# Early value products, block 1's x transposed by DMA, q's weights loaded once: a transformer block on one core

## The chip, the core and the metric

The kernel runs on one core of one Trainium2 chip. The metric is device time in microseconds (us) of one execution; lower is better. A run with more than 1.5% over the fastest of its kernel counts as slow and is left out of comparisons. "Profile" below is one execution recorded by the hardware profiler; its span is a little shorter than the device time of the same execution (731.3 for 733.04 us in the main one below). Engines: PE (TensorE, matmuls), DVE (VectorE), ACT (ScalarE), POOL (GpSimd), SP (SyncE, here only issuing transfers).

## The reference, cut to what matters

```python
x  = A_x                                   # 1 x 2048 x 1024, bf16
xn = layernorm(x)
qkv = xn @ wqkv                            # 1024 x 3072, 32 heads of 32
# position s attends to s, s-2, ..., s-14   (W, dil = 8, 2), masked below 0
s  = attention(q, k, v) @ wo
h  = silu(xn @ w1) * (xn @ w3)             # 1024 -> 3584
g  = silu(h @ w2)                          # 3584 -> 1024
return x + s * g
```

## The kernel before

The 2048 positions are four **blocks** (0 to 3) of 512, and two of them make a half (b = 0, 1). Every large product is one level of a Strassen-like scheme, seven products in place of eight, so operands have to be summed and differenced first, on DVE. The program is written in dependency order with priorities; a scheduler fixes each engine's order when the kernel is built, and each engine works through its own list in that order.

The order of the main parts: layer norm and transposes of x; q, k, v of half 0; q, k, v of half 1; up-projection, down-projection and output projection of half 0 ("am", "da" to "de", "wa" in the profile); then the same of half 1. Attention of the four blocks is DVE work that the scheduler fits in beside PE.

The start, with block 1's transposes on PE (`ln_tp`) and copied out by ACT:

```python
b12 = k4("b12", (KH, CH), BF16)
x_load(2)
ln_dve(1, [0, 1])
ln_dve(1, [2, 3])
...
def tp1(*sts):
    for st in sts:
        ln_tp(1, st, [(b12[:].unsqueeze(1), slice(0, 1)), (xT[:, 2:3], slice(1, 2))])

for t, (w0, w1_, ws) in enumerate(((wq0, wq1, sq), (wk0, wk1, sk))):
    first_two(f"f{t}", ...,                # the first two of the seven products
              *((lambda: None, 4) if t == 0 else (lambda: tp1(2, 3), 0)))
    if t == 0:
        tp1(0, 1)
qkv_sums(wq0, wq1, sq)
xn_sums(xT[:, 0], xT[:, 1], b12[:], xT[:, 2], xs)     # needs block 1 transposed
```

```python
def c22(gp):                               # after each of two groups of product "de"
    sp5 = k4(f"dsp{b}_{gp}")
    act_copy(sp5[:], pe[gp][:])
    with hp():
        anchor["v"] = nc.vector.tensor_add(sp5[:], pb[gp][:], sp5[:])
        silu(g_tile(b, 1, 1, gp), sp5[:])

product(pe, lst(s1), rhs, True, c22)
product(pe, lst(s4), rhs, False, c12)      # accumulates on top of what c22 copied out
```

The second product on `pe` may not write a group before ACT has copied that group out. In ACT's queue, group 0's silu, which needs DVE's sum, stands before group 1's copy.

## Time and profile before

| what | before |
|---|---|
| device time, three runs | 733.41 us median (731.72 to 733.42) |
| span of the profile, granted clock | 730.3 us, 0.998 |
| PE busy | 714.2 us, 98% |
| PE's first q product to its first "eq" product | 13.25 to 29.57 us |
| half 1's up-projection starts ("am") | 529.79 us |
| last output projection starts ("wa") | 699.88 us |

How to read it: PE is the engine to shorten. This is the timeline of the kernel before, all engines, of the half-1 down-projection (start, length, engine, line, operation, output<-inputs, shape, count; in brackets the idle time ahead of it and what ended it):

```profile
649.13 1.17 POOL L387 COPY vT<-vT 128x64 bf16<-128x64 bf16 x1 [16.27 <-DVE BC L465]
650.60 0.77 POOL L401 DMA_DIRECT2D vT<-v_dram  x1 [0.30 <-POOL vT L387]
...
658.30 1.23 DVE L465 TENSOR_TENSOR oT<-Ep,vT 128x2048 bf16<-128x2048 bf16 x1 [4.65 <-DMA vT<-v_dram]
...
675.70 12.25 PE L149 MATMUL de<-wring,h_sb 128*128 128x512 bf16 x54
...
678.35 1.22 DVE L814 TENSOR_TENSOR dsp<-db,dsp 128x1024 f32<-128x1024 f32 x1
...
679.60 1.06 ACT L777 ACTIVATE h_sb<-dsp 128x1024 bf16<-128x1024 f32 x1 [8.73 <-DVE dsp L814]
680.57 0.99 ACT L159 COPY dsp<-de 128x1024 f32<-128x1024 f32 x1
```

PE runs the second "de" product from 675.70 without a break: 54 of its 56 matmuls are recorded (one record is missing in each group of 28). The first group's last matmul starts 27 x 0.216 = 5.83 us later, at 681.53, and the second group is due one pitch after it, at 681.75 us; ACT's copy of that group ends at 680.57 + 0.99 = 681.56. So no wait is recorded, yet the **slack**, the time between "free" and "due", is only 0.19 us.

### The profile page before, as it was taken

To read this page: it belongs to the slowest core of one execution; us is meant where nothing else is said; L and a number is where in the kernel's file an instruction comes from. 1 tells how busy PE (TensorE), PEld (TensorE's weight loads), DVE (VectorE), ACT (ScalarE), POOL (GpSimd) and SP (SyncE) were. 2 spreads that over 40 slices of the span, in tenths; PEclk is the share of its full clock that TensorE was granted. 3 is DMA by queue.
4 is the path that set the end of the run, shared out by engine and by line. 5 is a ranking of instruction groups with operands and counts; after the bars stand their busy time and mean duration, and the time that the engine had idled before them with its cause. 6 is when DMAs were issued, how large, how long until landed. Compare 5 with 4: busy or idle time off the path is not lost.

```text
span 730.3 us, 8739 instructions
## 1 busy us (share of the span) xinstructions
PE 714.2 (98%) x3312; PEld 345.8 (47%) x3367; DVE 624.2 (85%) x677; ACT 314.5 (43%) x328; POOL 99.3 (14%) x159
## 2 busy tenths in 40 slices
PE   7999999999999999999999999999999999999996
PEld 4655665654444444444444444444444444444442
DVE  7994688878798879878989899969859999979984
ACT  5744343437554546654545411123454555120233
POOL 0000000010400110142202010010345000510011
PEclk9999999999999999999999999999999999999999
DMA  9379148877756452467755745549799453666505
GB/s 321 140 177 286 57 147 281 254 210 262 200 204 231 143 175 87 141 194 242 231 174 191 240 156 186 178 162 375 188 283 326 136 159 102 192 190 203 179 5 111
DMA packets 117610, 140.82 MB, mean 193 GB/s; under 512 B 14273, under 2 KB 91073, under 8 KB 116929
## 3 DMA queue, kind: packets, MB, share of 16 engines
q1 hardware_dynamic: 103984, 101.47, 44.9%
q0 software_dynamic: 13584, 38.81, 17.2%
q8 instruction: 26, 0.43, 0.3%
q14 instruction: 16, 0.12, 0.1%
HBM read 98.30 MB, written 38.80 MB: 188 GB/s over the span
## 4 chain that ended last, share of the span: by engine, by line
PE 71%; DVE 18%; DMA 4%; issue 3%; ACT 3%; SPq 1%; POOL 0%; DVEq 0%; ACTq 0%; POOLq 0%
PE bm L149 17%; PE am L149 11%; PE em L149 11%; PE db L149 7%; PE bq L149 5%; PE de L149 4%; DVE pt L410 4%; PE eq L149 4%; PE da L149 3%; PE aq L149 3%; PE wb L149 2%; DVE pt L412 2%; PE we L149 2%; PE wa L149 2%; DMA q_dram<-pk 1%
## 5 line engine op out<-in xcount | busy, mean ns | idle before, releaser
L149 PEld LDWEIGHTS <-wring 128*128 128x128 f16 (+1 forms) x1920 | 201.7, 105 | 216.4 <-issue 5.2
L149 PEld LDWEIGHTS <-h_sb 128*128 128x128 f16 (+1 forms) x1088 | 114.0, 105 | 121.7 <-issue 1.0
L149 PE MATMUL bm<-xs,wring 128*128 128x512 f16 x504 | 117.3, 379 | 0.5 <-DVE h_sb L661 0.3
L149 PE MATMUL am<-xT,wring 128*128 128x512 bf16 x322 | 78.8, 379 | 0.9
L410 DVE TENSOR_TENSOR pt<-qt,kT 128x4096 bf16<-128x4096 bf16 x32 | 73.2, 2288 | 0.7
L149 PE MATMUL db<-wring,h_sb 128*128 128x512 f16 x336 | 73.2, 379 | 0.0
L465 DVE TENSOR_TENSOR BC<-Ep,vT 128x2048 bf16<-128x2048 bf16 x56 | 67.0, 1218 | 0.2
L646 DVE TENSOR_TENSOR um<-em,um 128x1024 f32<-128x1024 f32 x28 | 34.2, 1222 | 19.9 <-PE em L149 12.9
L648 ACT ACTIVATE g<-um 128x1024 bf16<-128x1024 f32 x28 | 29.6, 1057 | 49.7 <-DVE um L646 49.7
L149 PE MATMUL da<-wring,h_sb 128*128 128x512 bf16 x219 | 48.9, 379 | 0.3
L451 POOL DMA_DIRECT2D Ep<-pb x64 | 37.9, 600 | 25.5 <-DVE pb L447 18.5
L149 PE MATMUL bm<-h_sb,wring 128*128 128x512 f16 x168 | 39.7, 379 | 0.0
L149 PE MATMUL em<-xs,wring 128*128 128x512 f16 x168 | 39.7, 379 | 0.0
L412 DVE TENSOR_TENSOR pt<-pt 128x2048 bf16<-128x2048 bf16 x32 | 39.1, 1221 | 0.5
L475 DVE TENSOR_TENSOR oT<-oT,BC 128x2048 bf16<-128x2048 bf16 x32 | 39.1, 1220 | 0.5
L149 PE MATMUL em<-xT,wring 128*128 128x512 bf16 x161 | 39.2, 379 | 0.3
L159 ACT COPY bm<-am 128x1024 f32<-128x1024 f32 x28 | 28.0, 999 | 26.1 <-PE am L149 26.1
L159 ACT COPY pm<-em 128x1024 f32<-128x1024 f32 x28 | 28.4, 1013 | 19.3 <-PE em L149 19.2
L159 ACT COPY um<-bm 128x1024 f32<-128x1024 f32 x28 | 28.4, 1013 | 18.6 <-PE bm L149 18.2
L667 ACT CAST g<-bm 128x1024 bf16<-128x1024 f32 x28 | 28.3, 1010 | 17.6 <-PE bm L149 17.6
L351 DVE TENSOR_TENSOR pk<-eq,uq 128x1024 bf16<-128x1024 f32 x12 | 14.7, 1222 | 23.7 <-PE eq L149 13.2
L661 DVE TENSOR_TENSOR h_sb<-bm,pm 128x1024 bf16<-128x1024 f32 x21 | 25.6, 1218 | 5.3 <-PE bm L149 5.3
(176 smaller groups left out, 965.3 us busy)
## 6 DMA issues: line engine op xcount, KB each, us to landing
wring<-in_B_w_dram SPq DMA_DIRECT2D x61, 512.0 KB, 4.4
wring<-t_dram SPq DMA_DIRECT2D x16, 512.0 KB, 5.1
t_dram<-wring POOLq DMA_DIRECT2D x14, 512.0 KB, 4.5
wring<-in_A_wqkv_dram SPq DMA_DIRECT2D x6, 1024.0 KB, 8.0
wring<-t_dram SPq DMA_DIRECT2D x16, 384.0 KB, 5.5
wring<-in_B_w_dram SPq DMA_DIRECT2D x12, 384.0 KB, 4.7
wring<-in_A_x_dram SPq DMA_DIRECT2D x16, 256.0 KB, 6.1
Ep<-pb POOLq DMA_DIRECT2D x64, 64.0 KB, 4.9
```

Source lines behind the costliest of these rows:

```text
L149: anchor["pe"] = nc.tensor.matmul(ps, lhsT=lhs[k], rhs=rhs[k], start=(first and k == 0), stop=(k == n - 1), skip_group_check=not first,)
L159: nc.scalar.copy(out=out_, in_=in_)
L351: anchor["v"] = nc.vector.tensor_add(d, ps[:], a[0][:])
L410: nc.vector.tensor_mul(p_t[:], q[:], kT[:, :, o:o + CH])
L412: nc.vector.tensor_add(p_t[:, 0:4, :], p_t[:, 0:4, :], p_t[:, 4:8, :])
L451: nc.gpsimd.dma_start(out=pr[c][r:P:NR, :, sq * P:(sq + 1) * P], in_=pb[sq * 32:(sq + 1) * 32, :, :])
L465: nc.vector.tensor_mul(dst, E[:, w, :].unsqueeze(1).to_broadcast([P, n, CH]), vT[:, js, o:o + CH])
L475: nc.vector.tensor_add(A, A, B if w0 else C)
L646: v = nc.vector.tensor_add(su2[:], pe[:], su2[:])
L648: nc.scalar.activation(out=hl["g"][:, :, CH:], in_=su2[:], func=ACTF.Silu)
L661: anchor["v"] = nc.vector.tensor_add(h[:, :, CH:], pb[:], sp5[:])
L667: nc.scalar.copy(out=hl["g"][:, :, 0:CH], in_=pb[:])
```

## The change

Intent: give PE the transposes of block 1 back (they go to DMA, straight from normalised rows to both halves of the transposed x), and fill the time in which DVE still waits for them with the first two value products of half 0. For that v's weights must be loaded at the start; they then stay until half 1. So do q's, which saves loading those a second time (6 loads of 1 MB of q, k and v weights where there were 8; v's were loaded once before too). The core of the diff:

```diff
-    def qkv_sums(w0, w1_, st):
+    def qkv_sums(w0, w1_, st, again=False):      # again: three sums where four were
@@ park: block 1's q, k, v go to DRAM on POOL's queue
-            nc.sync.dma_start(out=dst, in_=tl[:])
+            (nc.gpsimd if c == 1 else nc.sync).dma_start(out=dst, in_=tl[:])
@@ scores: block 0's scratch lies in oT
-            sc[c] = att_tile((W, CH), BF16, f"Es{c}"), att_tile((NJ, CH), BF16, f"pt{c}")
+            sc[c] = att_tile((W, CH), BF16, f"Es{c}"), oT[:, 0] if c == 0 else att_tile((NJ, CH), BF16, f"pt{c}")
@@ slots of the weight ring, in the order in which the up-projection takes them
-    free = [0, 1, 2, 3, 4, 6, 7, 8, 9]
+    free = [8, 9, 0, 1, 4, 2, 3, 6, 7]
@@ start
+    wve = [att_tile((4, D), BF16, f"wve{h}") for h in I]
+    vsn = att_tile((2, 2, CH), FP32, "vsn")
-    b12 = k4("b12", (KH, CH), BF16)
+    b12 = rows(12, 2).rearrange("p (k n) -> p k n", k=KH)
+    TPE = ()                                     # row groups transposed on PE: none
+    qkv_load(2, 0, wve[0][:])
+    for st in range(NST):
+        ln_dve(1, [st])
+        if st not in TPE:
+            for a, d in ((0, b12), (1, xT[:, 2])):
+                nc.sync.dma_start(
+                    out=d[:, :, st * P:(st + 1) * P], in_=xt[1][:, st, a * CH:(a + 1) * CH], transpose=True,
+                )
+        if st == 1:
+            qkv_load(2, 1, wve[1][:])
     x_load(2)
-    ln_dve(1, [0, 1])
-    ln_dve(1, [2, 3])
...
-    for t, (w0, w1_, ws) in enumerate(((wq0, wq1, sq), (wk0, wk1, sk))):
+    snap += [vsn[:, 0], vsn[:, 1]]
+    for t, (w0, w1_, ws) in enumerate(((wq0, wq1, sq), (wk0, wk1, sk), (wve[0][:], wve[1][:], sk))):
...
-    qkv_seven(2, 0, *wv, sv, step0)
+    qkv_seven(2, 0, *wv, sv, step0, snap[4:6])
...
-    wq0 = qkv_load(0, 0, slot(8, (4, D)))
-    wq1 = qkv_load(0, 1, rows(0, 4).rearrange("p (k n) -> p k n", k=4))
-    qkv_sums(wq0, wq1, sk)
+    qkv_sums(wq0, wq1, sk, True)
```

More of the change, by code (lines that the diff above doesn't have):

```diff
@@ L315, in qkv_sums @@
         s3 = hi(w0.bitcast(FP16))
+        if again:
+            nc.vector.tensor_sub(s2, a22, s3)
+            nc.vector.tensor_add(s1, s2, a11)
+            nc.vector.tensor_sub(s4, a12, s2)
+            pace["owed"] += 3.4
+            return
         nc.vector.tensor_add(s1, a21, a22)
@@ L993, in tp1 @@
         for st in sts:
-            ln_tp(1, st, [(b12[:].unsqueeze(1), slice(0, 1)), (xT[:, 2:3], slice(1, 2))])
-    for t, (w0, w1_, ws) in enumerate(((wq0, wq1, sq), (wk0, wk1, sk))):
+            ln_tp(1, st, [(b12.unsqueeze(1), slice(0, 1)), (xT[:, 2:3], slice(1, 2))])
+    snap += [vsn[:, 0], vsn[:, 1]]
+    for t, (w0, w1_, ws) in enumerate(((wq0, wq1, sq), (wk0, wk1, sk), (wve[0][:], wve[1][:], sk))):
         first_two(f"f{t}", [qkv_A(w0, w1_, ws, g) for g in range(2)], B0[0], B0[1],
                   snap[2 * t:2 * t + 2], [qkv_copy(t, 0, 2 * g) for g in range(2)],
-                  *((lambda: None, 4) if t == 0 else (lambda: tp1(2, 3), 0)))
-        if t == 0:
-            tp1(0, 1)
+                  *((lambda: None, 4) if t == 0 else (lambda: None, 0)))
+    tp1(*TPE)
     qkv_sums(wq0, wq1, sq)
-    xn_sums(xT[:, 0], xT[:, 1], b12[:], xT[:, 2], xs)
+    xn_sums(xT[:, 0], xT[:, 1], b12, xT[:, 2], xs)
     qkv_sums(wk0, wk1, sk)
@@ L1012 @@
     tr(2)
-    wv = [slot(2 + 4 * h, (4, D)) for h in I]
+    wv = [wve[h][:] for h in I]
     sva = slot(0, (2, 4, CH), FP16)
@@ L1019, in before_v @@
         if g == 0:
-            for h in I:
-                qkv_load(2, h, wv[h])
             tr(3)
-        else:
             with behind("v"):
```

## The prediction

> **What bounds the kernel now.** I read the page first, its busy shares and slices, then the table of stretches, then PE's own waits, then the timeline of the first 75 us, the only place where the change moves much.
>
> ```profile
> PE 714.2 (98%) x3312; PEld 345.8 (47%) x3367; DVE 624.2 (85%) x677; ACT 314.5 (43%) x328; POOL 99.3 (14%) x159
> ...
> PE   7999999999999999999999999999999999999996
> ...
> DMA  9379148877756452467755745549799453666505
> ```
>
> PE is at 9 in every slice but the first and the last. DVE is full in places (49.28 of 50.00 us from 420 to 470), but PE is at 49.90 there, so DVE fills PE's time without setting it. PE's waits over the whole run, as the waits view names them:
>
> ```profile
> PE tp L280 <- DVE wring L254: 2.3, 1, 2.3
> PE warm L141 <- DVE warm L138: 1.3, 1, 1.3
> PE am L149 <- ACT bm L159: 0.7, 1, 0.7
> PE eq L149 <- DVE xs L294: 0.5, 1, 0.5
> PE zp L425 <- DVE dsu L823: 0.5, 1, 0.5
> PE bq L149 <- DVE pk L351: 0.3, 1, 0.3
> PE bm L149 <- DVE h_sb L661: 0.3, 1, 0.3
> ```
>
> That is all there is to recover by waiting less: about 3.6 us at the start (two rows the change doesn't touch), some 2.5 us elsewhere. The rest of any gain must come from PE work removed. The chain of waits is no guide here: from 143 us on it runs through transfers and DVE, while PE is busy for 37.77 of the 39.00 us from 143 to 182. So the question is what PE does between 13 and 40 us:
>
> ```profile
> 13.25 7.07 PE L149 MATMUL af<-xT,wring 128*128 128x512 bf16 x32
> 20.15 1.06 PE L280 MATMUL tp<-ident,wring 128*128 128x128 bf16 x16
> 21.04 3.62 PE L149 MATMUL af<-xT,wring 128*128 128x512 bf16 x15
> 24.50 1.06 PE L280 MATMUL tp<-ident,wring 128*128 128x128 bf16 x16
> 25.40 3.62 PE L149 MATMUL af<-xT,h_sb 128*128 128x512 bf16 x16
> 29.57 2.35 PE L149 MATMUL eq<-xs,h_sb 128*128 128x512 f16 x10 [0.54 <-DVE xs L294]
> ```
>
> The columns are start, length, engine, line, operation. One row of q products (32), one half of block 1's transposes, half of k's products (16; one record is missing), the other transposes, the rest of k's, and then a wait for the differences of x (xs), which need the transposed block 1.
>
> **What the Trainium skill says.** "TensorE: Matmul & The Clock Gate", Part 4 (PE-mode transpose): a transpose on TensorE is a matmul against the identity whose output lands in PSUM, so a copy must follow; about 275 ns in one kernel's context. The trace shows the copies (eight on ACT, about 0.6 us each) but not the price: 219 ns for one, and pipelined 0.89 us for sixteen by their starts (20.15 to 21.04), 56 ns each. "DMA: Bandwidth & Descriptors", Latency and other measured facts: a DMA transpose at 261 GB/s in one kernel. Agrees: from 60.7 to 62.7 us the later blocks' transposes alone move 271 GB/s; one of 256 KB takes 1.32 us to issue and 3.0 to 8.2 us to land. The same page, Issuing engines are not separate DMA queues: issuing from another engine saves only sequencer time. Here that is what is wanted: SP's queue is held for 29.3 us in six waits for DVE pk before 100 us, and what stands behind such a wait is held too. "SBUF — State Buffer", SBUF: two separate sides: while DVE runs in a two-port mode GpSimd can't write descriptors, so DMAs issued there may start late. The trace shows no harm: POOL's t_dram DMAs land in 4.5 us, SP's 512 KB weight loads in 4.4.
>
> **The change, part by part.** The instruction orders of the two builds give the counts.
>
> (a) Block 1's transposes leave PE: 3367 matmuls become 3335, the 3248 of 128x512 stay. 0.89 + 0.90 (24.50 to 25.40) = 1.79 us off PE's stream, all on the path. ACT loses the eight copies, 4.9 us, off the path.
>
> (b) First v products placed early: 32 matmuls (A11 B11 and A12 B21 for two groups) move to before the first eq products. Count unchanged; what they do is cover the wait for xs. The matmul pitch is 0.216 us (eight from 33.59 to 35.32). Before: 64 products x 0.216 = 13.82, plus 1.79, leaves 16.32 - 15.61 = 0.71 us lost between 13.25 and 29.57. That is the 0.54 of the view and a pipeline refill. After: 96 x 0.216 = 20.74, so eq would start at 13.25 + 20.74 = 34.0 us; the like point before is 29.57 + 32 x 0.216 = 36.5. Gain of (a) and (b) 2.5 us, if nothing new waits.
>
> (c) What must be there in time. DVE's order up to the first xs holds one more 128x2048 operation (pitch 1.14 us) and one bn_stats (0.6) less than before, so xs L294 comes about 0.5 us later, 28.8 instead of 28.29; each of the next three takes 1.13. DMA: the seven loads of 1 MB (x0, wq twice, x1, wk twice, v's first half) at the 390 GB/s of the timeline end near 2.2 + 18.4 = 20.6 us. Then a half of the transposes (0.5 MB at about 215 to 271 GB/s, 2.2 us), v's second half (2.7 us), the other half of the transposes: about 28 us, landing by 30. v's second half lands near 27 and is needed at 13.25 + 80 x 0.216 = 30.5; xs is done at 31 and needed at 34. Margins of 3 us, on estimates. The DMA queues were idle in these microseconds before (1 GB/s from 28 to 38 us), which is why I believe them.
>
> (d) PSUM. In the new ACT order the two q copies that free the first two accumulators stand behind a k copy which waits for k's third group of eight, done at 13.25 + 56 x 0.216 = 25.3. Copies of about 0.95: k until 26.3, q until 27.3. The first v product is due at 27.1 and needs that accumulator: 0.3 us of wait.
>
> (e) q and v weights loaded once, four of q's sums rebuilt with three: 2 MB less traffic at 112 to 122 us, and one DVE operation (1.14 us) less. Neither engine is the bound there; PE loses 0.27 us from 110 to 143. Worth 0 to 0.2 us.
>
> (f) Block 1's parks move to POOL's queue, b12 leaves the small pool: DVE's 6.4 us wait at 62 us for a k_dram landing should go, and with it PE's 0.3 at 65 us. Worth 0.3 us.
>
> (g) The reordered slot list, the scores' scratch in oT, v's snapshot in the attention pool: no PE work. They move DVE's fill-in work a few operations and could cost or give half a microsecond where act tables load (PE loses 1.2 us from 143 to 182).
>
> Sum: -1.8 - 0.7 + 0.3 - 0.3 = -2.5, and 0.1 back for (g): 733.4 - 2.4 = 731.0 us.
>
> **The rivals.** First, the transposes land late. Issue time could do it: eight of 128 KB through one sequencer, each waiting for its own normalised rows, and an issue took up to 3.3 us[...] (54.5 us). Then v's second half, queued behind four of them, lands after 30.5, or xs after 34, and PE waits 1 to 3 us: 731.5 to 734. For it: that 3.3 us and the 8.2 us landing. Against: by 21 us the bulk is through. Second, the gain is hidden: DVE becomes the bound in the next stage, because it starts the later blocks' layer norm no earlier than before (x block 2 is now issued after the transposes, from 26 us instead of 10). Against: DVE idles 7.9 us between 29.6 and 64. Would make 733. Third, the attention pool: four long tiles fill it, so the first scores wait for v's snapshot and block 1's q for v's weights. If DVE's attention work slipped by 10 us or more, PE would wait before the output projection. Against: the snapshot is read near 77 us and the first score came at 89.6; v's weights are done near 127, and before, q's fetch was held in POOL's queue by parks until about 147. I give it 7%; it would make 735 to 740. Fourth, upwards: fewer collisions at 115 to 180 us return another microsecond, 729.5.
>
> **Range and chances.** The runs before spread over 1.7 us by themselves, so the range is the sum of that and of the rivals: 728.5 to 734.0. Two per cent is 14.7 us; all of PE's waits together are less than that, so faster by over 2% is next to impossible, 1%. Slower by as much needs a stall that no view hints at, 2%.
>
> **What would show it.** In the changed profile: PE matmuls down by 32; no PE transposes after 12 us; the first eq product at 34 us (late transposes: a PE wait for xs or the wve tiles there, 35 or later); a PE wait of about 0.3 us at 27 us ended by ACT; DVE's wait for the k_dram landing gone; the stretch from 182 us on as long as before within half a microsecond. The prediction is wrong if the eq start is right but the end isn't 2 to 3 us earlier (lost again in a later stage), or if DVE waits for the transposes.

## More of the kernel before

The attention's last step. A key and a value window reach back into the block before, so before a new block is fetched over the old one, the last columns are copied to the front (`halo`):

```python
def halo(t, js):
    nc.gpsimd.tensor_copy(out=t[:, js, 0:HALO], in_=t[:, js, CH:CH + HALO])

def fetch_v(c, js):
    if c == NC:
        return
    halo(vT, js)
    anchor["pool"] = nc.gpsimd.dma_start(out=vT[:, js, HALO:], in_=v_dram[c, :, js])

def values(c):
    ...
    for h in range(NJ // n):               # two halves of the channels
        js = slice(n * h, n * h + n)
        A = oT[:, c % 2, js]
        for w0 in range(0, W, 2):
            pvmul(B if w0 else A, w0)      # A, B, C <- weight * shifted v
            pvmul(C, w0 + 1)
            if w0:
                nc.vector.tensor_add(B, B, C)
            nc.vector.tensor_add(A, A, B if w0 else C)
        fetch_v(c + 1, js)
        if h == 0 and c % 2 == 0:
            fetch_k(c + 2)
```

(The yields that hand control back to the scheduler are cut.)

Attention of block 3 runs during the down-projection of half 1 and has to be complete before the last output projection.

## The result, and the profile after

| | runs | median us | lowest to highest | ratio to before | 95% |
|---|---|---|---|---|---|
| before | 6 | 733.3 | 731.72 to 733.47 | | |
| changed | 6, one slow | 735.05 | 733.82 to 755.1 | 1.0032 | 1.001 to 1.0054 |
| before, measured again | 11 | 732.89 | 731.75 to 734.89 | | |
| changed, measured again | 6 | 733.96 | 733.04 to 735.07 | 1.0014 | 0.9999 to 1.0029 |

A ratio is the mean time of one kernel's fast runs over that of the other's fast runs of the same rounds, so it is not quite the ratio of the medians quoted. The change is "the same" within 2%; at finer scale it is 1 to 2 us slower, where 2.4 us faster had been predicted. The first profile of the changed kernel fell in the slow state (755.1 us, granted clock 0.947), so all readings below are from the profile of the second measurement: span 731.3 us, clock 0.997. Its page:

```profile
PE 714.5 (98%) x3281; PEld 344.8 (47%) x3335; DVE 622.7 (85%) x678; ACT 313.5 (43%) x324; POOL 111.7 (15%) x171
...
PE   8999999999999999999999999999999999999896
```

Against the page before: 31 fewer matmuls on record, and yet 0.3 us more PE time; and one 8 has appeared among the 9s, in the third slice from the end.

**The start did what was predicted.** PE's timeline of the changed kernel:

```profile
12.32 10.30 PE L149 MATMUL af<-xT,wring 128*128 128x512 bf16 x47
22.68 3.62 PE L149 MATMUL af<-xT,h_sb 128*128 128x512 bf16 x16
26.13 7.07 PE L149 MATMUL af<-xT,wve 128*128 128x512 bf16 x32
33.04 1.89 PE L149 MATMUL eq<-xs,h_sb 128*128 128x512 f16 x8
```

96 products from 12.32 to 33.04 take 20.72 us; 20.74 had been worked out. The kernel before needed 16.32 us and had 32 of these products still ahead of it, 32 x 0.216 = 6.91 us: 23.23 in all. The gain is 2.51 us; 2.5 was predicted. (That the first product starts 0.93 us earlier than before is not the change: in the other profiles with the changed start it began at 12.2 to 13.6 us, in those with the old start at 12.3 to 13.3.)

**The gain is still there at 526 us, and gone at 701.**

| us in the profile | first q product | first eq | am, half 1 | wa, half 1 | end of span |
|---|---|---|---|---|---|
| before | 13.25 | 29.57 | 529.79 | 699.88 | 730.3 |
| changed | 12.32 | 33.04 | 526.37 | 701.07 | 731.3 |

At "am" of half 1 the changed kernel is 3.42 us ahead: 2.51 from the start, 0.93 from the head start, nothing lost between. From there to "wa" it takes 174.70 us where the kernel before takes 170.09. The whole result is in these 4.6 us. PE's waits over the changed run (engine, line, what it waited for: us in total, times, longest):

```profile
PE de L149 <- ACT dsp L159: 3.0, 1, 3.0
PE bq L149 <- DVE pk L357: 1.9, 3, 1.1
PE warm L141 <- DVE warm L138: 1.3, 1, 1.3
```

The first row is new, and it is a single wait. The timeline of the changed kernel at that place, for the same instructions as shown of the kernel before:

```profile
646.55 4.57 POOL L393 COPY vT<-vT 128x64 bf16<-128x64 bf16 x1 [30.43 <-DVE BC L471]
651.42 0.77 POOL L407 DMA_DIRECT2D vT<-v_dram  x1 [0.30 <-POOL vT L393]
...
658.95 1.23 DVE L471 TENSOR_TENSOR oT<-Ep,vT 128x2048 bf16<-128x2048 bf16 x1 [7.92 <-DMA vT<-v_dram]
...
672.06 6.21 PE L149 MATMUL de<-wring,h_sb 128*128 128x512 bf16 x27
678.00 1.22 DVE L820 TENSOR_TENSOR dsp<-db,dsp 128x1024 f32<-128x1024 f32 x1
679.25 1.06 ACT L783 ACTIVATE h_sb<-dsp 128x1024 bf16<-128x1024 f32 x1 [12.01 <-DVE dsp L820]
680.21 0.99 ACT L159 COPY dsp<-de 128x1024 f32<-128x1024 f32 x1
681.26 7.89 PE L149 MATMUL de<-wring,h_sb 128*128 128x512 bf16 x27 [2.99 <-ACT dsp L159]
```

Read from the bottom. PE's second group is held 2.99 us for ACT's copy. The copy stands in ACT's queue behind a silu that waits for DVE's sum (678.00), and the sum stands in DVE's queue behind the products with v. DVE had stood still for 7.92 us at 651, for a piece of v out of DRAM. That piece was asked for at 651.42, after POOL's halo copy, which began 2.58 us earlier than before and took 3.40 us longer. Set side by side: PE arrives 3.64 us earlier than before (672.06 for 675.70), while DVE's multiply starts 0.65 us later and its sum only 0.35 us earlier. So the chain by way of DVE had come earlier along with PE, up to the halo copy, and lost its lead there. With a copy 3.40 us shorter the group would have been free at 677.80, before it was due at 678.11 (an estimate from these lines).

The last group shows a second loss: 7.89 us for 27 matmuls, where the group before took 6.21. The first six keep the pitch of 0.216 us, the next eight are about 0.43 us apart (682.55 to 685.92), the rest 0.216 again. So the stop costs 2.99 + 1.68 = 4.67 us, against the 4.61 that the milestones show. The table of stretches (us, PE busy and count, weight loads, DVE, ACT, POOL, granted PE clock, DMA share, GB/s) has it too, for the kernel before and then the changed one:

```profile
655.00:700.00 45.00, 44.90 (x208) 20.47 (x209) 40.50 (x35) 7.05 (x7) 0.00 (x0) 1.00 0.52 169
```

```profile
655.00:702.00 47.00, 43.86 (x194) 19.52 (x196) 41.82 (x36) 7.89 (x8) 0.00 (x0) 0.96 0.42 136
```

The clock granted over the stretch falls from 1.00 to 0.96 beside the wait. The Trainium skill, "TensorE: Matmul & The Clock Gate", table under "Why this matters for your kernels", says to have no idle gap over about 3 us between matmul bursts, or throughput drops. The runs here agree on the size, though not without exception. In the fast profiles no wait of PE up to 2.46 us is followed by a lower clock. Of the eleven waits of 2.71 us and more, ten have half the clock granted beside them, for 3.41 us (6.83 in two); in the changed kernel it is 0.50 from 682.6 to 685.9 us. The eleventh, of 3.00 us in the run with the value products late, has not.

### The profile page after: what moved, and what is told of

The parts are those of the page before. It is cut to its first block, busy times and chain, and to the rows that moved or that the text cites. A ratio compares the mean times of both kernels' runs of the same rounds, so it can differ in the third digit from the quotient of the medians.

```text
span 753.4 us, 8729 instructions
## 1 busy us (share of the span) xinstructions
PE 743.8 (99%) x3335; PEld 349.8 (46%) x3335; DVE 624.1 (83%) x678; ACT 313.6 (42%) x324; POOL 111.7 (15%) x171
## 4 chain that ended last, share of the span: by engine, by line
PE 84%; DVE 6%; issue 5%; DMA 3%; ACT 1%; POOL 1%; SPq 0%; DVEq 0%; POOLq 0%
PE bm L149 18%; PE am L149 13%; PE em L149 13%; PE bq L149 8%; PE db L149 7%; PE eq L149 5%; PE de L149 4%; PE da L149 3%; PE af L149 3%; PE aq L149 3%; PE wb L149 2%; PE we L149 2%; DMA vT<-v_dram 2%; PE wa L149 2%; DVE BC L471 2%
## 5 line engine op out<-in xcount | busy, mean ns | idle before, releaser
L149 PEld LDWEIGHTS <-wring 128*128 128x128 f16 (+1 forms) x1824 | 191.3, 105 | 220.4 <-issue 2.5
L149 PEld LDWEIGHTS <-h_sb 128*128 128x128 f16 (+1 forms) x1056 | 111.2, 105 | 126.9 <-issue 1.4
L149 PE MATMUL bm<-xs,wring 128*128 128x512 f16 x504 | 122.1, 390 | 0.0
L149 PE MATMUL am<-xT,wring 128*128 128x512 bf16 x336 | 82.8, 390 | 0.0
L149 PE MATMUL db<-wring,h_sb 128*128 128x512 f16 x336 | 76.2, 390 | 0.0
L416 DVE TENSOR_TENSOR pt<-qt,kT 128x4096 bf16<-128x4096 bf16 x24 | 55.0, 2290 | 0.7
L149 PE MATMUL da<-wring,h_sb 128*128 128x512 bf16 x224 | 51.0, 391 | 0.0
L149 PE MATMUL em<-xT,wring 128*128 128x512 bf16 x168 | 41.3, 391 | 0.0
L149 PE MATMUL em<-xs,wring 128*128 128x512 f16 x168 | 41.3, 391 | 0.0
L956 POOL DMA_DIRECT2D out_dram<-h_sb x12 | 15.1, 1512 | 101.5 <-DVE h_sb L955 101.5
```

Of the source, the lines that this page charges most:

```text
L149: anchor["pe"] = nc.tensor.matmul(ps, lhsT=lhs[k], rhs=rhs[k], start=(first and k == 0), stop=(k == n - 1), skip_group_check=not first,)
L416: nc.vector.tensor_mul(p_t[:], q[:], kT[:, :, o:o + CH])
L956: nc.gpsimd.dma_start(out=rows_, in_=g, accum_op=ALU.add)
```

## The experiments

**Theory A**: in the late stage PE is tied to DVE's order. DVE takes the first v product of block 3's second channel half (the one that writes straight into oT) before the rest of the first half, and so stands idle for v's fetch with runnable work behind it; the fetch waits for POOL's halo copy. The kernel before had no slack there, so any gain ahead of it is lost. (This last step did not hold as it stands: the slack was 0.19 us, and the stop comes to kernels that arrive late as well; see the table below.) **Rival theories**: the loss belongs to the new start (the DMA transposes, or the parks moved to POOL's queue, disturb later transfers); or the halo copy, slower in the changed kernel, is all of it; or the loaded-once weights and the slot order cost PE time by themselves.

### The changed kernel again

No edit; it gave the profile above.

> The changed kernel unaltered, to get a profile in the fast state and a tighter time: the one profile there is fell in the slow state (granted clock 0.947), yet shows PE with no wait over 0.7 us. Theory 1 (denser PE work is throttled more): in a fast profile PE still has almost no gaps, matmul pitch times count accounts for the span, and the granted clock is below the 0.998 of before, with about 4 to 5 us of stretched pitch. Theory 2 (a new wait that the slow state's slower PE hid): the clock is 0.998 as before, the front is 2 to 2.5 us ahead at 40 us, and PE gaps of 4 to 5 us in all appear later, beside a full DVE. Theory 3 (noise of six runs): the ratio over five rounds is 1.000 or below.

Measured: 733.96 us, ratio 1.0014 (0.9999 to 1.0029). The loss against the prediction repeats. Theory 2 fits the profile: the clock is 0.997 and the gap is a late one, 2.99 us, beside a full DVE. In the first, slow profile PE waits 0.66 us at the same place.

### Block 1's transposes back on PE, all else as changed

```diff
-    TPE = ()
+    TPE = (0, 1, 2, 3)
```

> The changed kernel with block 1 transposed on PE again (32 more matmuls of 128x128, 1.8 us of PE), all else as changed. If the DMA transposes are harmless, this is 1.5 to 2 us slower than the changed kernel. If they cost (late xs, or SP's queue held for 29 us so that later loads and transposes slip), it is the same or faster than the changed kernel.

Measured: 741.55 us, ratio 1.011 (1.0093 to 1.0127), 7.6 us over the changed kernel. PE's timeline:

```profile
34.26 1.95 PE L280 MATMUL tp<-ident,wring 128*128 128x128 bf16 x32
40.93 3.56 PE L149 MATMUL eq<-xs,h_sb 128*128 128x512 f16 x8 [4.73 <-DVE xs L294]
```

The transposes themselves cost 1.95 us at most, as priced. But here they stand at the end of the early products, and nothing is left to cover the way through the copies and DVE's differences: 4.73 us of wait, and eight matmuls that take 3.56 us for 1.89. 1.95 + 4.73 + 1.67 = 8.4, of which 7.6 reach the end. The DMA transposes do not cause the loss; without them this arrangement is far worse.

The late stop is in this profile too:

```profile
655.03 4.57 POOL L393 COPY vT<-vT 128x64 bf16<-128x64 bf16 x1 [30.40 <-DVE BC L471]
689.99 7.61 PE L149 MATMUL de<-wring,h_sb 128*128 128x512 bf16 x27 [3.23 <-ACT dsp L159]
```

PE begins its second "de" pass 8.5 us later here than in the changed kernel (680.55 for 672.06), and is held all the same, because DVE's sum comes 8.7 us later too (686.73 for 678.00). So it is not an early PE that makes the stop: the chain by way of DVE moves with PE, and what counts is the distance between the two.

### Block 1's parks back on SP's queue

```diff
-            (nc.gpsimd if c == 1 else nc.sync).dma_start(out=dst, in_=tl[:])
+            nc.sync.dma_start(out=dst, in_=tl[:])
```

> The changed kernel with block 1's twelve parks back on SP's queue. If POOL's queue is what costs (parks in order ahead of t_dram stores and of the fetches of k and q), this is 2 to 5 us faster than the changed kernel. If the move was worth what the prediction gave it (0.3 us), it is the same within 0.5 us or slightly slower, and DVE waits for a k_dram landing again.

Measured: 734.2 us, ratio 1.0011 (0.9991 to 1.0031). No difference from the changed kernel is seen, and the profile has the same late wait (3.17 us). The rival of the parks falls. Whether moving them is worth the 0.3 us that the prediction gave it, a measurement with an interval of about 1.5 us to either side can't tell.

### The value products late again

```diff
-    for t, (w0, w1_, ws) in enumerate(((wq0, wq1, sq), (wk0, wk1, sk), (wve[0][:], wve[1][:], sk))):
+    for t, (w0, w1_, ws) in enumerate(((wq0, wq1, sq), (wk0, wk1, sk))):
...
-    qkv_seven(2, 0, *wv, sv, step0, snap[4:6])
+    qkv_seven(2, 0, *wv, sv, step0)
```

> The changed kernel with block 0's first v products not placed early (all else as changed, block 1 still transposed by DMA). The prediction gave the early products 0.7 us, as the cover of the wait for xs that the kernel before had. Theory A says they cover far more: in the changed kernel xs is done at 33 us or later, and without the 32 products PE would arrive at 26 us, so PE should idle some 6 us before the first eq and the time should rise by 5 to 8 us over the changed kernel. If the prediction's sizing is right, it rises by about 1 us.

Measured: 743.72 us, ratio 1.0137 (1.01 to 1.0174), 9.8 us over the changed kernel. PE's timeline:

```profile
32.72 3.60 PE L149 MATMUL eq<-xs,h_sb 128*128 128x512 f16 x8 [5.93 <-DVE xs L294]
36.11 2.75 PE L149 MATMUL bq<-xs,h_sb 128*128 128x512 f16 x8
```

5.93 us of wait and (3.60 - 1.89) + (2.75 - 1.89) = 2.57 us of slow matmuls are 8.5 of the 9.8; the rest is open. The early value products are not worth 0.7 us, as the prediction had it, but 8 to 10: without them the DMA transposes would lose time. The two parts only pay together. The late stop is here as well: 3.00 us, though PE begins its second "de" pass at 682.53, 10.5 us later than in the changed kernel.

### DVE's order mended, in the changed kernel and in the kernel before

The second half's first product goes into the working buffer B, as all later ones do, so that it can't be taken early; the sum then starts the accumulator:

```diff
-                pvmul(B if w0 else A, w0)
+                pvmul(B if w0 or h else A, w0)
 ...
-                nc.vector.tensor_add(A, A, B if w0 else C)
+                if w0:
+                    nc.vector.tensor_add(A, A, B)
+                elif h:
+                    nc.vector.tensor_add(A, B, C)
+                else:
+                    nc.vector.tensor_add(A, A, C)
```

> The changed kernel, with the first multiply of each second half of the value products written to the scratch B instead of straight to oT, so that DVE's order can no longer put it ahead of the first half (same operations, same count). Theory A (the front gain is lost late: in block 3, DVE stands idle 7.9 us for the second half of v behind that multiply, and PE then waits 3.0 us for an ACT copy that waits for DVE, and runs about nine matmuls at half pace): DVE's wait for vT at 651 us is gone, PE's wait in the last projection is gone, and the time falls by 4 to 4.6 us, to 729.5. Rival B (the loss is spread over many small collisions of the reordered slots and parks): under 1.5 us of difference.

Measured, in the changed kernel: 729.22 us, ratio 0.9951 (0.9932 to 0.997). The same edit in the kernel before:

> The same edit on the kernel before. Theory A: DVE's idle time of 4.65 us before the last fetch of v goes, but PE does not wait there, as the copy it needs ends just when PE arrives (681.56 us), so the time stays within 0.5 us of before. Rival B' (the edit is a gain by itself, nothing to do with the change): it gains as much here as on the changed kernel.

Measured: 733.35 us, ratio 1.0014 (0.9989 to 1.0038). The edit takes DVE's idle time for v away in both, but pays only where PE was held: nothing in the kernel before, whose "de" never waited, and 0.63% (the difference of the ratios, 4.6 us) in the changed one. The arithmetic is the same, and so is the number of instructions; only the order moved. This was run once more for confirmation (the same chip number, 14, so it was not another chip):

> order_after once more, unaltered: the version that beats both kernels, to confirm its time on another chip and to get a profile of its usual run (the first profile was of its slowest run). Expected 729 to 730, ratio 0.993 to 0.997 to before, no PE wait in the last projection, and a wait of 1 to 2 us near 161 us that stays.

Measured: 730.74 us (729.34 to 732.4), ratio 0.9958 (0.9945 to 0.9972). Its late stage, all engines:

```profile
650.88 5.71 POOL L393 COPY vT<-vT 128x64 bf16<-128x64 bf16 x1 [29.96 <-DVE BC L471]
656.88 0.77 POOL L407 DMA_DIRECT2D vT<-v_dram  x1 [0.30 <-POOL vT L393]
...
674.43 1.22 DVE L825 TENSOR_TENSOR dsp<-db,dsp 128x1024 f32<-128x1024 f32 x1
...
676.27 12.25 PE L149 MATMUL de<-wring,h_sb 128*128 128x512 bf16 x54
676.64 0.99 ACT L159 COPY dsp<-de 128x1024 f32<-128x1024 f32 x1
```

The halo copy is longer still (5.71 us) and v's fetch 5.46 us later than in the changed kernel, and it harms nobody: DVE has other work until v lands. DVE's sum comes 3.57 us earlier (674.43 for 678.00), the copy ends at 677.63, and PE wants the group at 682.32. That is 4.7 us of slack where the changed kernel was 3.1 us short; the same edit in the kernel before leaves 4.7 us as well, where 0.19 had sufficed. A caution: this profiled execution was the slowest of its five, held near 160 us (below). As DVE's chain moves with PE, read the slack and the medians, not the times of the clock.

### The halo copy moved to ACT

```diff
     def fetch_v(c, js):
-        halo(vT, js)
+        nc.scalar.copy(out=vT[:, js, 0:HALO], in_=vT[:, js, CH:CH + HALO])
```

> The changed kernel with the 64-column halo copies of v made by ACT instead of POOL. On POOL the last of these copies took 4.57 us (1.17 in the kernel before). Theory A in its second half (the late fetch is that stretched copy): the fetch is issued some 4 us earlier, DVE's wait for vT falls from 7.9 to about 4, PE's wait goes and the time falls by 3 to 4.6 us. If the copy's length is beside the point, the wait and the time stay.

Measured: 730.99 us (729.25 to 733.39), ratio 0.9971 (0.9948 to 0.9994). The fetch goes out at 650.70 (651.42 in the changed kernel), DVE waits 3.16 us instead of 7.92, and the group of "de" is free at 680.07, 1.7 us before it is due (681.75). This copy takes 0.24 us on ACT. So a short halo copy alone takes the stop away, and the time falls by 0.43% of the kernel before (3.2 us, the difference of the ratios). PE was held for 2.84 us near 161 us in this profile and came late to the stage, but so did DVE's chain, as in the two kernels above that come later still and stop. With both mends together:

> order_after and the halo copies of v on ACT together. With the order mended, DVE no longer stands before the late fetch, so the halo copy should not matter any more: within 1 us of order_after. A further gain of over 1 us would say that the fetch still held something.

Measured: 730.76 us (729.64 to 731.96), ratio 0.9961 (0.9943 to 0.998). Not told apart from the order alone: once DVE doesn't stand on the fetch, the copy's length no longer counts.

### The halo copy made long in the kernel before

The opposite dose: in block 3's fetch of the kernel before, the same copy is done four times.

```diff
-        halo(vT, js)
+        for k in range(4 if c == 3 else 1):
+            halo(vT, js)
```

> The kernel before, with the halo copies of v for block 3 made four times (the same bytes again), which doubles the suspected cost there. Theory A says the kernel before has no slack at that point: three more copies of at least 1.2 us delay the fetch by 3.5 us or more, PE waits about as long at the last projection, and the time rises by 3.5 to 6 us. If the kernel before has slack there, it rises by less than 1 us.

Measured: 737.4 us, ratio 1.0071 (1.0044 to 1.0097): 4 to 5 us lost. Its timeline:

```profile
649.18 4.69 POOL L387 COPY vT<-vT 128x64 bf16<-128x64 bf16 x4 [16.69 <-DVE BC L466]
...
661.63 1.22 DVE L466 TENSOR_TENSOR oT<-Ep,vT 128x2048 bf16<-128x2048 bf16 x1 [7.85 <-DMA vT<-v_dram]
...
684.94 7.89 PE L149 MATMUL de<-wring,h_sb 128*128 128x512 bf16 x27 [2.99 <-ACT dsp L159]
```

A copy 3.5 us longer makes in the old kernel the stop of the new one, to the digit: 2.99 us, then 7.89 us for 27 matmuls. Nothing of the change is in this kernel. It shows that the place had next to no slack before, that v's fetch sets it, and that a longer copy ahead of that fetch is enough to make the stop.

The late stages in one table. "Starts" is the start of PE's second "de" pass, "due" comes 28 pitches of 0.216 us after it, "free" is the end of ACT's copy:

| kernel | halo copy, us | starts | due | free | PE's wait |
|---|---|---|---|---|---|
| before | 1.17 | 675.70 | 681.75 | 681.56 | none recorded |
| changed | 4.57 | 672.06 | 678.11 | 681.20 | 2.99 |
| changed, transposes on PE | 4.57 | 680.55 | 686.59 | 689.93 | 3.23 |
| changed, value products late | 4.57 | 682.53 | 688.57 | 691.69 | 3.00 |
| before, four halo copies | 4.69 | 675.74 | 681.79 | 684.88 | 2.99 |
| changed, halo on ACT | 0.24 | 675.70 | 681.75 | 680.07 | none |
| changed, order mended (second run) | 5.71 | 676.27 | 682.32 | 677.63 | none |
| before, order mended | 1.17 | 675.17 | 681.21 | 676.54 | none |

PE goes on at whichever of "due" and "free" is later. (The recorded waits are a little shorter than the difference of the two, because a matmul's recorded end lies 0.16 us past the next one's start.) The column "starts" does not sort the kernels that stop from those that don't. The copy's length does as long as the order is unmended, and with the order mended the length no longer counts. So the stop takes two things: DVE's order, which left 0.19 us, and a halo copy 3.4 us longer.

### A second, smaller place: 160 us

In the order-mended kernel five of the six runs were at 728.86 to 729.28 us and one, the profiled one, at 732.82. That profile has a wait of 2.71 us near 161 us, "bq" for DVE's pk; the second measurement's has 2.93, the changed kernel's 1.07. DVE in turn waits for the landing of a park: in the changed kernel,

```profile
158.37 1.22 DVE L357 TENSOR_TENSOR pk<-eq,uq 128x1024 bf16<-128x1024 f32 x1 [5.28 <-DMA q_dram<-pk]
```

POOL issues the 1 MB fetch of block 1's k at 150.70 us there, at 157.58 in the kernel before, so it now shares the DMA engines with q's parks. To test that, the fetch was put later, with its halo copy on DVE (the order mend is in this kernel too):

```diff
-            fetch_k(c + 1)
+            if c:
+                fetch_k(c + 1)
             hooks.append(lambda: score_sums(c))
             yield STOP
+            if not c:
+                fetch_k(c + 1)
```

> order_after with the fetch of block 1's k held back until q's last DVE sum (its halo copy moved to DVE, behind that sum). There is a second wait of the changed kernel at 161 us, of 1.1 to 2.8 us by profile: PE waits for a DVE sum that waits for a park's landing, while the 1 MB fetch of k, now issued at 151 us instead of 158, shares the DMA engines. If that fetch is the cause, the wait goes (below 0.4 us) and the time falls by 1 to 2 us below order_after, to 727.5 to 728.5. If not, the wait stays, and DVE's later scores may even cost something.

Measured: 734.28 us, ratio 1.0012 (0.9998 to 1.0025): a miss as a remedy. PE's waits for pk are gone (0.6 us at most), which fits the cause (the halo copy of k went to DVE in the same edit, so the time of the fetch is not the only difference), but the k that comes later is now waited for in its turn; DVE's line, then PE's:

```profile
177.79 2.29 DVE L419 TENSOR_TENSOR pt<-qt,kT 128x4096 bf16<-128x4096 bf16 x1 [5.97 <-DMA kT<-k_dram]
```

```profile
181.27 3.57 PE L149 MATMUL bm<-xs,wring 128*128 128x512 f16 x8 [3.81 <-DVE h_sb L678]
```

PE loses more there than it gained. A fetch time between the two, or another buffer for the parks, was not tried.

### The old slot order

```diff
-    free = [8, 9, 0, 1, 4, 2, 3, 6, 7]
+    free = [0, 1, 2, 3, 4, 6, 7, 8, 9]
```

in the order-mended kernel.

> order_after with the slot list in its old order. The prediction gave the new order no PE time. Kept q weights lie in slots 2, 3, 6 and 7 until q is done at 158 us; with the old order the first weights of the next stage are assigned to slots 2 and 3 and must wait for that. If the new order is a needed part of loading q once, PE waits for a weight load near 160 us and the time rises by 2 us or more; if it is only tidiness, it stays within 0.7 us.

Measured: 735.98 us, ratio 1.0027 (1.0008 to 1.0047): 5 to 7 us over the order-mended kernel's two medians. PE's timeline:

```profile
167.73 1.90 PE L149 MATMUL em<-xs,wring 128*128 128x512 f16 x8 [1.98 <-DVE wring L612]
```

DVE can't build the first up-projection sums in a slot that q's weights still hold, now that these stay until half 1. The new list, which looked like bookkeeping, is what makes loading q once affordable. The wait shown is 2.0 us of the 5 to 7; the profiled run was the fastest of its four (732.88 us; the others took 735.65 to 736.37), and the rest was not traced.

## Why the prediction was wrong

By its own steps:

- **(a) and (b), the start: the sum was right** (2.5 predicted, 2.51 measured). The split was not. The 0.7 us for the early value products is the term that was mis-sized: it was read from the kernel before, where PE transposes stood between the products and left 0.7 us of wait. With DMA transposes the wait to be covered is 5.93 us, and with the slow matmuls behind it 8.5.
- **(c), what must be there in time: right in the result, tight in the size.** DVE stood for 2.82 us and its first difference came at 30.89 instead of 28.8 (the waits view names no releaser; the view of the transposes' line puts these 2.8 us down to them, and the last pair was issued from 26.69). So "DVE waits for the transposes", one of the prediction's signs of being wrong, did come. PE saw nothing of it, but the difference was ready at 32.12, 0.9 us before PE took it and not 3. The first rival did not come in this profile; in three others (parks on SP, old slots, both mends) PE waited 0.4 to 1.0 us near 31 us for v's second half. Two readings behind these estimates were off: 271 GB/s was the rate from 62.7 to 64.6 us (from 60.7 to 62.7 it was 226), and seven loads of 1.05 MB at 390 GB/s take 18.8 us, not 18.4.
- **(d), 0.3 us for PSUM at 27 us: absent.** There is no wait of PE between 12.32 and 33.04.
- **(e), weights loaded once: not isolated by any run, and a need overlooked.** (g) said of the slot list "no PE work", at most half a microsecond. Without it the time is 5 to 7 us worse.
- **(f), the parks: 0.3 us predicted, no difference found** (734.2 against 733.96), nor could one so small be seen. DVE's wait for the k_dram landing is gone, as predicted.
- **What failed** is the step from the start to the end: the reading that "DVE fills PE's time without setting it", with (g)'s "half a microsecond" for DVE's moved work, and the check drawn from it, "the stretch from 182 us on as long as before within half a microsecond". From "am" to "wa" of half 1 the changed kernel takes 4.61 us longer. There DVE does set PE's time: its sum had let ACT's copy end 0.19 us ahead of PE before. In the changed kernel POOL's halo copy takes 4.57 us for 1.17, DVE stands 7.92 us for 4.65 behind the fetch that follows it, and PE stops for 2.99 us and loses 1.68 more at the lower clock. The list of waits was taken as "all there is to recover by waiting less", which is true, and silently also as all the places where PE could be held, which is not: no wait may mean next to no slack.
- **The rivals.** The third looked at the right place, "PE would wait before the output projection", but expected a slip of DVE's attention work by 10 us or more, from the attention pool, and gave 7%. A slip of 3.3 us against PE was enough (DVE's sum 5.94 us after the start of PE's pass where it had been 2.65), and it came from the halo copy. The prediction's last sentence named the outcome that came, "the eq start is right but the end isn't 2 to 3 us earlier (lost again in a later stage)", without a place for it and without weight in the range.
- **The range**, 728.5 to 734.0, missed the first median, 735.05, and holds the second, 733.96, only at its edge. That it would be within 2% was right. With the one place mended the same change is at 729.2 to 730.7, faster than both kernels and where the prediction had put it or slightly below.

Shown by the runs: the late stop, its cause in DVE's order and v's late fetch, the part of the halo copy's length in it, and the 0.19 us of slack in the kernel before. Not shown: why the halo copy of one and the same shape took 1.17 us in the three profiles of kernels with the old start, 4.57 in the five of the changed kernel with DVE's order unmended and 5.71 in the four with it mended (copies on POOL). The length goes with the build; whether DVE's order or something else that differs sets it is open. The lengths are about one, four and five of DVE's instructions at their pitch of 1.14 us, and the copy runs beside DVE's back-to-back multiplies and sums; an earlier copy of the same shape, at 606.15 us in the kernel before, took 0.24 us. What decides how many it loses to was not tested.

## What to carry to other kernels

Look at every later hand-over to the bound engine for its slack (when the result is ready against when it is wanted), not only at the recorded waits: 0.19 us of slack showed as no wait, and a copy 3.4 us longer somewhere behind it swallowed the whole gain. Compare such times against the bound engine's own, not by the clock of the profile, for here the other engines' work came earlier and later with it. An engine that stands on a transfer with runnable work queued behind it is often mended by order alone; here, by sending one product to a scratch buffer instead of an accumulator that happened to be free. And price a part of a change in the arrangement that the change makes, for here two parts together gained 2.5 us at the start, and with either one undone the kernel was 8 to 10 us slower than before (ratios 1.011 and 1.0137, the late stop included).

## What the Trainium skill lacked or had wrong

- "TensorE: Matmul & The Clock Gate", Why this matters for your kernels: the limit of about 3 us of idle agrees in size. Here it lies between 2.46 us (no effect) and 2.71 us of recorded wait, with one wait of 3.00 us that had no effect. One such gap cost 6 to 13 matmuls of 128x512 at 0.43 us instead of 0.216, 1.4 to 2.7 us, on top of the wait.
- The same page, Part 4 (PE-mode transpose): about 275 ns each in a kernel's context, in transpose mode. The kernel here transposes by plain matmuls against an identity: one is recorded with 219 ns, and 32 pipelined ones take 1.95 us, 61 ns each, so the figure is not the price in a stream of them. The wait for what follows them, 4.73 us, was the larger cost.
- "SBUF — State Buffer", SBUF: two separate sides: the lock between DVE with two SBUF inputs and a GpSimd operation that reads SBUF would fit a 64-column GpSimd copy that took 0.24 us once and 1.17, 4.57 and 5.71 us beside DVE's two-input multiplies. The page speaks of the loser waiting until the other instruction ends; if that lock is the cause, the copy lost to four or five in a row, 1.14 us each. No run isolated it.
- "DMA: Bandwidth & Descriptors", Latency and other measured facts: that section has a rate for DMA transposes, but no issue time. In the changed kernel's trace the eight transposes of 128 KB took 1.2 to 2.8 us each to issue on SP and 3.3 to 8.6 us to land. The last pair went out from 26.69 us, 4.4 us after its rows were normalised (22.27), behind the issues ahead of it.
- No page that I read says how to look for hand-overs to a bound engine that have next to no slack and show no wait; the one here had 0.19 us and came to cost 4.6 us.
